# Attention ahead of a mixture of experts on one core: another order of a software pipeline's step, inverses in PSUM, routing by pairs of batches

## The chip, the cores and the metric

The kernel runs on one core of a Trainium2 chip. A core has five engines, each with its own queue that it works through in order: TensorE (PE in the profile, with its weight loads as PEld), VectorE (DVE), ScalarE (ACT), GpSimd (POOL) and SyncE (SP), which here only issues DMAs. The metric is the time on the device in microseconds for one execution, and a kernel's figure is the median over its runs.

## The reference

There are two stages. The first is attention over 8 batches and 8 heads, 576 positions of 64 elements: a local part, in which each position sees its neighbours at a distance under 4, and a pooled part, in which q, k and v are averaged over groups of four positions and the result is repeated four times. The second sends each of the 4608 rows of 512 elements to one of 8 experts.

```python
q_d, k_d, v_d = (t.reshape(B, H, S // 4, 4, D).mean(axis=3) for t in (q, k, v))
out_up = np.repeat(sm_attn(q_d, k_d, v_d), 4, axis=2)
scores = np.where(np.abs(pos[:, None] - pos[None, :]) < 4, scale * q @ k.T, -1e9)
attn = np.exp(scores - scores.max(-1))
attn = attn / (attn.sum(-1) + 1e-9)
x = rows_of(out_up + attn @ v)                   # 4608 x 512
logits = (x / |x|) @ (emb / |emb|).T / tau
e = argmax(logits);  gate = softmax(logits)[e]
out = gate * (relu(x @ w1[e]) @ w2[e])           # w1 512 x 1024, w2 1024 x 512
```

## The kernel before

**Attention** works in 32 units: a batch and a pair of heads, so that two heads of 64 fill 128 partitions. `attention` (line 179) is a software pipeline: in step i, unit a = i + 2 has its keys and queries transposed, unit c = i + 1 gets its scores and exponentials, unit d = i its transposed weights and its products with v, and unit e = i - 1 is turned back into rows. Each engine meets the work in the order in which the code issues it. Per step:

- `qk_T(a)`: 12 transposes on PE (L350) into four PSUM banks, and 8 copies on ACT (L354).
- `scores(c)`: the mask and 36 small products on PE (L383, L388) into one bank, the maximum and the difference on DVE (L394, L395), the exponential on ACT (L396). `scores_d(c)`: the pooled products (L405) into two banks, their maxima on DVE (L409), four exponentials on ACT that also leave their sums (L416).
- `pooled(a)`, `pooled_v(a)`: the sums of four on POOL (L368, L369, L377, L378).
- `weights_T(d)`: 9 transposes (L440) into three banks, copied by ACT (L443). `weights_dT(d)`: 8 transposes (L451) into two banks, copied by DVE (L453).
- `softmax(c)` on DVE: sums (L422), plus 1e-9 (L423), inverses (L424), all in SBUF.
- `rows(e)`: 5 transposes (L491), four into a bank of their own and the fifth into a bank called `shared`; ACT copies the four (L492); the products with the experts' embeddings (L496) into `shared`; DVE copies the fifth (L500) and adds the logits (L502, L504).
- `values_d(d)`: the pooled products with v (L460) into `shared`, copied by ACT (L466). `normalise(c)` on DVE: local weights times inverses (L430, two), pooled weights times inverses (L432). `values(d)`: 18 products with v (L476) into two banks, to which DVE adds the pooled part (L478, two).

All of PSUM is one pool of eight banks that go round: who wants a bank waits until the user eight banks ago has been read out. A step takes 16.

At the end of some steps a part of expert 0's weights is prepared (`first_weights`, line 781): squares on ACT (L748), two a step, or a split into two half-precision parts, ACT (L772) then DVE (L773).

When a batch's last unit is through, `place` (line 507) routes it, in parts that are spread over the following steps: `store` transposes the logits (L530, L531), scales them (L533), copies them into the rows (L534) and saves the rows to DRAM from SP (L519, L520); `pick` finds the first largest logit (L542 to L546); `rank` counts the rows ahead with products on PE (L551, L553) and works out each row's place (L558 to L566), from which POOL makes a table of ones (L568). In total 16 DVE operations a batch. After the first six batches three early slots of rows are gathered within the last steps (`early_slots`).

The loads go from SP, two units (half a batch) at a time: 8 DMAs for k and q (`load`, L316), 2 for v in the layout that is pooled (`load_v`, L325, one buffer), and 10 for v in overlapping windows of 70 positions (`load_w`, L334 for the 64 own rows of each head, L337 for the three rows on either side).

**The experts** (`run_slots`, line 931) work through slots of 128 rows with two products in half-precision parts, L1077 to L1079 and L1100 to L1102.

Of the kernel before, what the change touches and what calls it, by code (L numbers as in the profile page):

```python
# [21 lines left out]
NHP = H // 2  # L22
# [27 lines left out]
class Kern:  # L50
# [128 lines left out]
    def attention(self, ctx):  # L179
# [7 lines left out]
        for i in range(2):  # L187
# [3 lines left out]
            self.vw.append(z.tile([WV, G, 4, D], F32, name=f"vw{i}"))  # L191
            self.sums.append(z.tile([128, G + 4], F32, name=f"sums{i}"))
        self.lg = z.tile([TB, NTB, E + 1], F32, name="lg")
# [27 lines left out]
        for i in range(2):  # L221
            nc.vector.memset(self.kq[i][:, :, :3], 0.0)
            nc.vector.memset(self.kq[i][:, :, S + 3:], 0.0)
            nc.vector.memset(self.vw[i][:32, 0], 0.0)
            nc.vector.memset(self.vw[i][64:, G - 1], 0.0)
# [9 lines left out]
        for i in range(-2, n + 1):  # L235
# [6 lines left out]
            if 0 <= c < n:  # L242
                self.scores(st[c])
                if not c:
                    self.warm_up(3)
                self.scores_d(st[c])
# [8 lines left out]
            if 0 <= d < n:  # L255
                self.weights_T(st[d])
                self.weights_dT(st[d])
                if not d:
                    self.warm_up(7)
            if 0 <= c < n:  # L260
                self.softmax(st[c])
            yield i, 0
            self.shared, last_rows = self.bank(), None
            if mid:
                mid.pop()()
            if 0 <= e < n:
# [4 lines left out]
                last_rows = self.rows(st.pop(e), hp, *xr[b])  # L271
                if hp == NHP - 1:
                    for f in tail:
                        f()
                    tail = self.place(b, *xr.pop(b), mid)
            if 0 <= d < n:
                self.values_d(st[d], last_rows)
            elif last_rows:
                last_rows()
            if 0 <= c < n:  # L280
                self.normalise(st[c])
            if 0 <= d < n:
                self.values(st[d])
# [4 lines left out]
            if tail and i < n:  # L288
                tail.pop(0)()
# [949 lines left out]
```

## Time and profile before

| what | us |
|---|---|
| median of 3 runs | 784.87 (784.14 to 792.7) |
| the profiled execution | 789.27 |
| its span, first to last instruction | 787.6 |
| mean granted TensorE clock | 0.959 |

The profile is of one execution. Busy time counts the instructions of an engine; DMA issues, register and semaphore instructions are left out. The granted clock is the share of TensorE's full clock that it was given. Rows of the timeline give start, duration, engine, line, operation, written tile, read tiles, shape, count, and in brackets how long the engine had been idle before and what ended that. In a group by line, the number after the bar is the busy time, then the mean of one in ns, then the idle time before them. The chain of work that ended last reaches back only over the last 5 us here, so it says nothing of attention.

### The profile page before, as it was taken

The page shows a single profiled execution, that of the slowest core. Times are in us where ns is not written, and L with a number is a line of the kernel's source. Part 1 is how long each engine was busy: PE and PEld are TensorE (multiplying, and loading weights), DVE is VectorE, ACT ScalarE, POOL GpSimd, SP SyncE. Part 2 cuts the span into 40 slices and gives each one's busy share as a digit, 9 for nine tenths or more (in the row PEclk, how much of TensorE's full clock was granted, in tenths as well). Part 3 has the DMA queues.
Part 4 walks back from the last instruction along what each step waited for, and adds up shares of the span by engine and source line. Part 5 has one row for each costly group of instructions (what it writes and reads, how often), then busy time and mean ns, then how long its engine had stood idle before and what let it go on. Part 6 is the DMA issues. An engine that isn't in the chain of part 4 may idle for free. (4 is left out here: it accounts for less than half of the span.)

```text
span 787.6 us, 27918 instructions
## 1 busy us (share of the span) xinstructions
PE 723.7 (92%) x10540; PEld 547.2 (69%) x10540; DVE 508.8 (65%) x1503; ACT 517.0 (66%) x1159; POOL 408.4 (52%) x783
## 2 busy tenths in 40 slices
PE   7899898988998898889999999999999989999992
PEld 4677676767877677657677676777677767776771
DVE  7689799898799987945645647475654364456420
ACT  7698888798888864264754767577583366447510
POOL 7454657475465744726553564565655444525421
PEclk9899999899899978998999999999999999999997
DMA  8788898778789845622833737455553364337210
GB/s 182 144 203 192 194 215 152 222 147 233 135 187 187 169 133 171 184 56 77 254 88 123 192 81 241 120 176 163 189 175 83 83 162 155 83 92 221 60 39 17
DMA packets 160329, 117.77 MB, mean 150 GB/s; under 512 B 90514, under 2 KB 136594, under 8 KB 160160
## 3 DMA queue, kind: packets, MB, share of 16 engines
q1 hardware_dynamic: 152352, 94.55, 49.3%
q0 software_dynamic: 6560, 19.03, 7.9%
q10 hardware_dynamic: 1248, 2.11, 0.8%
q8 instruction: 85, 1.39, 0.8%
q14 instruction: 84, 0.69, 0.3%
HBM read 213.05 MB, written 20.33 MB: 296 GB/s over the span
## 5 line engine op out<-in xcount | busy, mean ns | idle before, releaser
L1077 PE MATMUL bank<-xT,w1h 128*128 128x128 f16 x1312 | 227.2, 221 | 11.1 <-DMA xT<-x 7.8
L1079 PE MATMUL bank<-xT,w1l 128*128 128x128 f16 x1312 | 227.1, 221 | 1.8 <-DVEq L921 1.6
L1078 PE MATMUL bank<-xT,w1h 128*128 128x128 f16 x1312 | 227.2, 221 | 0.0
L1077 PEld LDWEIGHTS <-w1h 128*128 128x128 f16 x1312 | 130.1, 99 | 18.7 <-DMA xT<-x 4.3
L1078 PEld LDWEIGHTS <-w1h 128*128 128x128 f16 x1312 | 130.2, 99 | 3.5
L1079 PEld LDWEIGHTS <-w1l 128*128 128x128 f16 x1312 | 130.1, 99 | 3.3 <-DVEq L921 1.9
L1102 PE MATMUL bank<-w2h,hT 128*128 128x512 f16 x328 | 124.3, 379 | 0.0
L1101 PE MATMUL bank<-w2l,hT 128*128 128x512 f16 x328 | 124.2, 379 | 0.0
L1100 PE MATMUL bank<-w2h,hT 128*128 128x512 f16 x328 | 124.2, 379 | 0.0
L354 ACT ACTIVATE kq<-bank 64x288 f32<-64x288 f32 x256 | 110.1, 430 | 15.4 <-PE bank L350 10.2
L1113 POOL DMA_INDIRECT out_dram<-o,ids x41 | 45.5, 1110 | 126.1 <-ACTq L916 91.9
L1089 DVE SCALAR_TENSOR_TENSOR hT<-bank,hT 128x512 f16<-128x512 f32 x82 | 55.3, 689 | 85.0 <-ACT hT L1088 49.9
L1088 ACT ACTIVATE hT<-bank 128x512 f16<-128x512 f32 x82 | 47.8, 595 | 88.2 <-PE bank L1079 74.8
L368 POOL TENSOR_TENSOR pool_kq<-kq 128x288 f32<-128x288 f32 x62 | 41.7, 680 | 74.0 <-ACT kq L354 71.6
L748 ACT ACTIVATE junk<-st 128x1024 bf16<-128x1024 f32 (+1 forms) x30 | 67.6, 2253 | 3.4 <-issue 2.2
L998 POOL DMA_INDIRECT xg<-xd,ids x41 | 45.5, 1109 | 43.3 <-issue 16.7
L1046 ACT ACTIVATE lg<-lg,lmx 128x8 f32<-128x8 f32 x41 | 12.4, 303 | 74.1 <-DVE lmx L1044 74.1
L377 POOL TENSOR_TENSOR pool_v<-ld_v 72x256 f32<-72x256 f32 x64 | 49.2, 780 | 19.5 <-DMA ld_v<-in_v_dram 17.9
L1102 PEld LDWEIGHTS <-hT 128*128 128x128 f16 x328 | 32.0, 98 | 38.8
L1100 PEld LDWEIGHTS <-hT 128*128 128x128 f16 x328 | 35.0, 107 | 33.9
L1028 DVE SCALAR_TENSOR_TENSOR x<-xg,sc,x 128x512 f16<-128x512 f32 x41 | 30.8, 751 | 40.5 <-ACT x L1025 40.4
L1101 PEld LDWEIGHTS <-hT 128*128 128x128 f16 x328 | 32.0, 97 | 33.9
(218 smaller groups left out, 1604.3 us busy)
## 6 DMA issues: line engine op xcount, KB each, us to landing
st<-in_moe_w_dram SPq DMA_DIRECT2D x148, 1024.0 KB
ld_k<-in_k_dram SPq DMA_DIRECT2D x64, 144.0 KB
ld_q<-in_q_dram SPq DMA_DIRECT2D x64, 144.0 KB
ld_v<-in_v_dram SPq DMA_DIRECT2D x32, 288.0 KB
vw<-in_v_dram SPq DMA_DIRECT2D x64, 144.0 KB
xd<-xr SPq DMA_DIRECT2D x8, 1040.0 KB
st<-in_moe_w_dram SPq DMA_DIRECT2D x12, 512.0 KB
st<-in_moe_w_dram ACTq DMA_DIRECT2D x4, 512.0 KB
```

Source lines behind the costliest of these rows:

```text
L354: nc.scalar.activation(out=kq[h * D:(h + 1) * D, w, 3 + r:3 + r + S:2], in_=ps[r * D:(r + 1) * D], func=AF.Copy, scale=(1.0, QS)[w])
L377: g.tensor_tensor(out=t6[:, c], in0=vr[:, :, 0:2 * D], in1=vr[:, :, 2 * D:], op=ALU.add)
L748: self.nc.scalar.activation(out=junk, in_=src, func=AF.Square, accum_out=acc)
L998: nc.gpsimd.indirect_dma_start(out=xg, out_offset=None, in_=self.xd[:n], in_offset=bass.IndirectOffsetOnAxis(ap=self.ids[:, q:q + 1], axis=0),
L1077: nc.tensor.matmul(out=o, lhsT=self.w1h[:, k, f], rhs=xT[:, 0, k], start=(k == 0), stop=False)
L1078: nc.tensor.matmul(out=o, lhsT=self.w1h[:, k, f], rhs=xT[:, 1, k], start=False, stop=False)
L1079: nc.tensor.matmul(out=o, lhsT=self.w1l[:, k, f], rhs=xT[:, 0, k], start=False, stop=(k == self.KC - 1))
L1088: nc.scalar.activation(out=h[:, 0], in_=ps, func=AF.Relu)
L1089: nc.vector.scalar_tensor_tensor(out=h[:, 1], in0=ps, scalar=0.0, in1=h[:, 0], op0=ALU.max, op1=ALU.subtract)
L1100: nc.tensor.matmul(out=ps, lhsT=hh, rhs=self.w2h[:, j, :], start=(j == 0), stop=False)
L1101: nc.tensor.matmul(out=ps, lhsT=hh, rhs=self.w2l[:, j, :], start=False, stop=False)
L1102: nc.tensor.matmul(out=ps, lhsT=hl, rhs=self.w2h[:, j, :], start=False, stop=(j == self.FC - 1))
```

## The change

- The order within a step. `scores` and `scores_d` now hold the products alone; the maxima and exponentials became `exps`, `peaks_d` and `exps_d`. PE does `weights_T(d)` before `scores_d(c)`. ACT copies the transposed weights (before: L443) ahead of the exponentials. After the row transposes, the order of DVE is: the row copies, `softmax`, the additions of `values`, and `normalise` last. ACT's copy of the rows (L492) comes after that of the pooled products (L466).
- PSUM: seven banks go round, and the eighth holds the inverses: the sums stay in SBUF, the sum plus 1e-9 and the inverse are written to PSUM, and `normalise` reads them there.
- Routing: for the first six batches `place` only does `store`, and every second batch `place_pair` does the rest for two batches at once, in seven parts, one a step (two a step in the four steps after batch 5). `store`'s copy into the rows, the products of `pick` and `rank` and one difference go to POOL. The parts are issued before the row transposes, where they stood at the end of the step.
- Loads of v: `load_v` is one DMA, `load_w` three (the own rows of four heads at once, and three rows on either side at once, in which rows of a neighbouring head come in where the weights are zero). The pooled positions are now split into even and odd ones instead of halves, so `weights_dT` reads every second column.

```diff
+            if 0 <= c < n:
+                self.scores_d(st[c])
+                self.exps(st[c])
+                self.peaks_d(st[c])
+            if 0 <= d < n:
                 self.weights_dT(st[d])
             if 0 <= c < n:
-                self.softmax(st[c])
+                self.exps_d(st[c])
             yield i, 0
-            self.shared, last_rows = self.bank(), None
             if mid:
                 mid.pop()()
+            for _ in range(2 if BEARLY * NHP <= i < (BEARLY + 1) * NHP else 1):
+                if tail and i < n:
+                    tail.pop(0)()
+            self.shared, parts = self.bank(), None
...
+            if 0 <= d < n:
+                self.values_d(st[d])
+            if parts:
+                parts[1]()
+            if 0 <= c < n:
+                self.softmax(st[c])
+            if 0 <= d < n:
+                self.out_d(st[d])
+                self.values(st[d])
+            if parts:
+                parts[0]()
...
             if 0 <= c < n:
                 self.normalise(st[c])
...
-        vr = ld.tile([CD, 2, 4, 4 * D], F32, name="ld_v", bufs=1)
-        for c in range(2):
-            nc.sync.dma_start(out=vr[:, c], in_=self.v[b, h, c * S // 2:(c + 1) * S // 2].rearrange(
-                "h (i r) d -> i h (r d)", r=4))
+        vr = ld.tile([CD, 4, 2, 4 * D], F32, name="ld_v", bufs=1)
+        nc.sync.dma_start(out=vr, in_=self.v[b, h].rearrange("h (i c r) d -> i h (c r d)", c=2, r=4))
...
-        for c in range(4):
-            own = bass.AP(g.tensor, g[c, 0:1].offset, [[D, 64], [64 * D, G], [1, D]])
-            nc.sync.dma_start(out=vw[3:WV - 3, :, c], in_=own)
-        for p, w0, t0 in [(r, 1, 61 + r) for r in range(3)] + [(WV - 3 + r, 0, 64 + r) for r in range(3)]:
-            edge = bass.AP(g.tensor, g[0, t0:t0 + 1].offset, [[D, 1], [64 * D, G - 1], [S * D, 4], [1, D]])
-            nc.sync.dma_start(out=vw[p:p + 1, w0:w0 + G - 1], in_=edge)
+        for p, np, f0, nf, t0 in ((3, 64, 0, n, 0), (0, 3, 1, n - 1, 61), (WV - 3, 3, 0, n - 1, 64)):
+            rows = bass.AP(g.tensor, g[0, t0:t0 + 1].offset, [[D, np], [64 * D, nf], [1, D]])
+            nc.sync.dma_start(out=vw[p:p + np, f0:f0 + nf], in_=rows)
...
-        nc.vector.tensor_scalar(out=sums, in0=sums, scalar1=1e-9, scalar2=None, op0=ALU.add)
-        nc.vector.reciprocal(out=sums, in_=sums)
+        inv = self.inv[:, s["u"] % 2]
+        nc.vector.tensor_scalar(out=inv, in0=sums, scalar1=1e-9, scalar2=None, op0=ALU.add)
+        nc.vector.reciprocal(out=inv, in_=inv)
...
-                nc.tensor.transpose(out=pt[:, i * CD:(i + 1) * CD], in_=s["ad"][:, i, c * CD:(c + 1) * CD],
+                nc.tensor.transpose(out=pt[:, i * CD:(i + 1) * CD], in_=s["ad"][:, i, c::2],
...
-            v.tensor_copy(out=xr[:, :, DM:], in_=lg[:, :, :E])
+            (v if b == B - 1 else nc.gpsimd).tensor_copy(out=xr[:, :, DM:], in_=lg[:, :, :E])
...
+        if b < BEARLY:
+            mid.append(store)
+            return self.place_pair(b - 1) if b % 2 else []
...
+    def place_pair(self, b0):
...
+        def best():
+            v.reduce_max(out=mx, in_=l8, axis=AX.X)
+            v.tensor_tensor(out=l8, in0=l8, in1=bc(mx), op=ALU.is_ge)
+            for i in range(2):
+                g.tensor_tensor(out=l8[:, i], in0=l8[:, i], in1=self.rev, op=ALU.mult)
+        def first():
+            v.reduce_max(out=mx, in_=lg, axis=AX.X)
+            v.tensor_tensor(out=oh[:, :, :NTB], in0=l8, in1=bc(mx), op=ALU.is_equal)
+        def rank(i):
...
+        def own():
+            for i in range(2):
+                g.tensor_tensor(out=rk[:, i], in0=rk[:, i], in1=oh[:, i, :NTB], op=ALU.mult)
...
+        def split():
+            v.reduce_sum(out=pos, in_=rk, axis=AX.X)
+            v.tensor_copy(out=posi, in_=pos)
+            v.tensor_scalar(out=posi, in0=posi, scalar1=SLOT - 1, scalar2=None, op0=ALU.bitwise_and)
+            v.tensor_copy(out=pm, in_=posi)
+            g.tensor_tensor(out=pb, in0=pos, in1=pm, op=ALU.subtract)
+            at(0)
+        return [best, first, lambda: rank(0), lambda: rank(1), own, split, lambda: at(1)]
...
-        self.bk = self.pool(ctx, "banks", 8, space=PSUM)
+        self.bk = self.pool(ctx, "banks", 7, space=PSUM)
+        self.inv = self.pool(ctx, "inverses", 1, space=PSUM).tile([128, 2, G + 4], F32, name="inv")
```

More of the change, by code (lines that the diff above doesn't have):

```diff
@@ L270, in attention @@
                              self.rt.tile([128, LW], F32, name="ls"))
-                last_rows = self.rows(st.pop(e), hp, *xr[b])
-                if hp == NHP - 1:
[L273 to L279, printed above, removed]
+                parts = self.rows(st.pop(e), hp, *xr[b])
+            if 0 <= d < n:
[9 more added lines that the diff above has]
+                parts[0]()
+                if hp == NHP - 1:
+                    while tail and b >= BEARLY:
+                        tail.pop(0)()
+                    tail += self.place(b, *xr.pop(b), mid)
+                    if b == B - 2:
+                        tail.pop(0)()
             if 0 <= c < n:
                 self.normalise(st[c])
-            if 0 <= d < n:
-                self.values(st[d])
             if i == -1:
@@ L374, in pooled_v @@
         t6 = wk.tile([CD, 2, 2, 2 * D], F32, name="pool_v", bufs=1)
-        for c in range(2):
-            vr = s["v"][:, c, j:j + 2]
-            g.tensor_tensor(out=t6[:, c], in0=vr[:, :, 0:2 * D], in1=vr[:, :, 2 * D:], op=ALU.add)
+        for h in range(2):
+            vr = s["v"][:, j + h]
+            g.tensor_tensor(out=t6[:, h], in0=vr[:, :, 0:2 * D], in1=vr[:, :, 2 * D:], op=ALU.add)
         g.tensor_tensor(out=vd, in0=t6[:, :, :, 0:D], in1=t6[:, :, :, D:], op=ALU.add)
@@ L497, in rows @@
                              start=True, stop=True)
+        def first():
+            nc.scalar.activation(out=dst[:, :4], in_=ps, func=AF.Copy)
         def rest():
@@ L504, in rest @@
                 nc.vector.tensor_copy(out=ls, in_=lg)
-        return rest
+        return first, rest
     def place(self, b, xr, ls, mid):
@@ L540, in pick @@
             l8 = lg[:, :, :E]
-            mx = rt.tile([TB, NTB], F32, name="lmx")
+            mx = rt.tile([TB, 2, NTB], F32, name="lmx2")[:, 0]
             v.reduce_max(out=mx, in_=l8, axis=AX.X)
@@ L575, in place, with bc, first, at @@
         return [take, pick, rank]
+    def place_pair(self, b0):
+        nc, rt = self.nc, self.rt
+        v, g = nc.vector, nc.gpsimd
+        bs = slice(b0, b0 + 2)
+        lg, oh = self.lg, self.oh[:, bs]
+        l8, shp = lg[:, :, :, :E], [TB, 2, NTB, E]
+        mx = rt.tile([TB, 2, NTB], F32, name="lmx2")
+        rk = rt.tile(shp, F32, name="rk2")
+        pos = rt.tile([TB, 2, NTB], F32, name="pos2")
+        posi = rt.tile([TB, 2, NTB], I32, name="posi2")
+        pm, pb = self.pm[:, bs], self.pb[:, bs]
+        def bc(x):
+            return x.unsqueeze(3).broadcast_to(shp)
+        def best():
[3 more added lines that the diff above has]
+                g.tensor_tensor(out=l8[:, i], in0=l8[:, i], in1=self.rev, op=ALU.mult)
+        def first():
+            v.reduce_max(out=mx, in_=lg, axis=AX.X)
+            v.tensor_tensor(out=oh[:, :, :NTB], in0=l8, in1=bc(mx), op=ALU.is_equal)
+        def rank(i):
+            pk, o = self.bank()[:, :(NTB + 1) * E].rearrange("p (t e) -> p t e", e=E), oh[:, i]
+            nc.tensor.matmul(out=pk, lhsT=self.tri, rhs=o, start=True, stop=False)
+            for t in range(1, NTB + 1):
+                nc.tensor.matmul(out=pk[:, t:], lhsT=self.onesb, rhs=o[:, :NTB + 1 - t], start=False,
+                                 stop=(t == NTB))
+            v.tensor_tensor(out=rk[:, i], in0=pk[:, :NTB], in1=self.base.unsqueeze(1).broadcast_to(shp[:1] + shp[2:]),
+                            op=ALU.add)
+            v.tensor_tensor(out=self.base, in0=self.base, in1=pk[:, NTB], op=ALU.add)
+        def own():
+            for i in range(2):
+                g.tensor_tensor(out=rk[:, i], in0=rk[:, i], in1=oh[:, i, :NTB], op=ALU.mult)
+        def at(i):
+            for t in range(NTB):
+                g.tensor_scalar(out=self.at[:, (b0 + i) * NTB + t], in0=self.iota, scalar1=pm[:, i, t:t + 1],
+                                scalar2=None, op0=ALU.is_equal)
+        def split():
[6 more added lines that the diff above has]
+        return [best, first, lambda: rank(0), lambda: rank(1), own, split, lambda: at(1)]
```

54 lines of the change are left out of this document (30 added, 24 removed).

## The prediction

> **What bounds the kernel now.** I read the page first, then the table of stretches, then the timeline of one step, then groups by line.
>
> ```profile
> span 787.6 us, 27918 instructions
> PE 723.7 (92%) x10540; PEld 547.2 (69%) x10540; DVE 508.8 (65%) x1503; ACT 517.0 (66%) x1159; POOL 408.4 (52%) x783
> ```
>
> TensorE is busy 92% of the span, but that is an average over two stages. The table below cuts attention at the starts of its steps (the first transpose L350 of a unit). The columns are span, then busy time and count of PE, PEld, DVE, ACT and POOL, then granted clock, DMA share and GB/s.
>
> ```profile
> 36.20:77.00 40.80, 38.00 (x846) 31.14 (x844) 36.49 (x101) 36.83 (x112) 18.93 (x27) 1.00 0.83 186
> 97.30:131.70 34.40, 30.67 (x679) 24.93 (x678) 31.79 (x87) 30.18 (x90) 23.28 (x30) 1.00 0.88 186
> 151.30:186.80 35.50, 30.86 (x682) 25.01 (x681) 32.51 (x84) 31.24 (x91) 21.70 (x28) 1.00 0.79 185
> 208.00:267.80 59.80, 53.17 (x1188) 43.26 (x1187) 54.80 (x150) 53.17 (x157) 35.14 (x50) 1.00 0.87 180
> 77.00:97.30 20.30, 17.09 (x342) 13.63 (x339) 15.13 (x41) 18.61 (x52) 12.27 (x18) 0.92 0.85 201
> 131.70:151.30 19.60, 18.62 (x343) 15.40 (x342) 16.35 (x42) 15.60 (x46) 8.75 (x13) 0.83 0.86 210
> 186.80:208.00 21.20, 19.65 (x343) 15.75 (x339) 15.02 (x42) 18.77 (x52) 13.31 (x19) 0.76 0.83 185
> 267.80:278.00 10.20, 8.63 (x170) 6.98 (x167) 9.66 (x25) 8.51 (x25) 8.93 (x9) 0.89 0.73 122
> 306.90:787.60 480.70, 452.29 (x5082) 330.52 (x5082) 248.38 (x787) 261.97 (x423) 229.97 (x520) 0.98 0.45 130
> ```
>
> From 306.9 us the experts run with PE busy 94%, and the change adds or removes nothing there but a PSUM bank. So the change acts on attention. The first four rows are 20 steps at full clock, 170.5 us or 8.5 each; the next four are 7 steps, 71.3 us, at a lower clock. At full clock no engine is full: ACT needs 7.4 a step (36.83 over 5), DVE 7.3 to 8.1, PE 7.6. A chain through all of them sets the step. Here is one, 8.23 us long, with only its carriers:
>
> ```profile
> 114.15 0.45 PE L350 MATMUL bank<-ident,ld_k 96*128 96x96 f32 x3
> 114.69 3.57 ACT L354 ACTIVATE kq<-bank 64x288 f32<-64x288 f32 x8 [0.66 <-PE bank L350]
> 115.23 0.81 DVE L478 TENSOR_TENSOR xT<-bank,od 128x320 f32<-128x320 f32 x2
> 116.19 0.71 PE L405 MATMUL bank<-kqd 64*72 64x144 f32 x8
> 116.83 1.18 PE L440 MATMUL bank<-ident,an 128*70 128x128 f32 x9
> 117.96 0.52 DVE L395 TENSOR_TENSOR a<-bank,mx 128x342 f32<-128x342 f32 x1
> 118.57 0.49 ACT L396 ACTIVATE a<-a 128x342 f32<-128x342 f32 x1 [0.30 <-DVE a L395]
> 119.08 0.38 ACT L416 ACTIVATE ad<-bank,md 72x144 f32<-72x144 f32 x1
> 119.97 0.33 PE L491 MATMUL bank<-ident,xT 128*128 128x128 f32 x1 [0.72 <-ACT ad L416]
> 120.53 1.24 ACT L443 ACTIVATE aT<-bank 70x384 f32<-70x384 f32 x3
> 121.23 1.22 PE L476 MATMUL bank<-aT,vw 70*64 70x64 f32 x36
> 121.92 1.73 DVE L430 TENSOR_TENSOR an<-a,sums 64x342 f32<-64x342 f32 x2
> 122.38 0.47 PE L350 MATMUL bank<-ident,ld_k 96*128 96x96 f32 x3
> ```
>
> Read it as a ring. L350 starts; 0.54 later ACT copies keys and queries for 3.57; ACT waits 0.30 for DVE; the exponentials of the local part and half of the pooled part take until 119.9 (118.57 on); then the fifth transpose L491 gets its bank, which those pooled exponentials were reading (0.72 of PE idle); from there PE runs on, 119.97 to 122.38, and the next L350 begins. The copies L443 stand behind the exponentials on ACT although PE had their data by 118.0 (L440).
>
> **The change, part by part.**
>
> *Order on ACT and banks.* L443 goes ahead of the exponentials, the pooled scores go behind the weight transposes on PE, and 7 banks rotate instead of 8. A step still takes 16 banks, so each waits for the one 7 uses back: the first bank of the weight transposes L451 now waits for the last L354, and the row transposes L491 for L443, done early. The new ring is L350, 0.54, L354 3.57, a semaphore (0.05), then PE alone from L451 to the next L350. An undisturbed stretch of that kind is in the trace:
>
> ```profile
> 300.46 0.67 PE L451 MATMUL bank<-ident,ad 72*72 72x72 f32 x8
> 302.61 1.22 PE L476 MATMUL bank<-aT,vw 70*64 70x64 f32 x36
> ```
>
> L451 to L476 is 2.15, and L476 to the next L350 1.15 (121.23 to 122.38) to 1.22: 3.4. So the ring is 0.54 + 3.57 + 0.05 + 3.4 = 7.6, against ACT's own 7.4. In a step with a piece of expert weights, ACT has one split more and is the bound.
>
> ```profile
> L748 ACT ACTIVATE junk<-st 128x1024 bf16<-128x1024 f32 x8 | 8.5, 1061 | 0.1
> L772 ACT ACTIVATE w1h<-st,wscl 128x1024 f16<-128x1024 f32 x4 | 4.7, 1166 | 0.0
> L773 DVE SCALAR_TENSOR_TENSOR w1l<-st,wscl,w1h 128x1024 f16<-128x1024 f32 x4 | 5.1, 1268 | 0.0
> L430 DVE TENSOR_TENSOR an<-a,sums 64x342 f32<-64x342 f32 x60 | 37.3, 621 | 0.4
> L395 DVE TENSOR_TENSOR a<-bank,mx 128x342 f32<-128x342 f32 x29 | 14.9, 515 | 1.0
> L543 DVE TENSOR_TENSOR lg<-lg,lmx 128x40 f32<-128x40 f32 x7 | 1.4, 200 | 0.2
> ```
>
> That is 7.4 + 1.1 = 8.45 rounded; DVE's 1.27 is then covered, since routing and L430 become cheaper (below). Of the 20 steps at full clock I count 15 plain, 5 with a split, and 1.6 us of PE waiting for its own instructions that I leave: 15 x 7.6 + 5 x 8.45 + 1.6 = 157.8, a gain of 12.7. The 7 others are held by a half clock or by two squares on ACT (2 x 1.061 a step), which stay; I take 0.4 each, half of a plain step's 0.9, so 2.9. Together 15.6.
>
> *Inverses in PSUM, normalisation last.* L430 had two SBUF operands and averages 621 ns; L395, as wide with one operand in PSUM, 515. L430 stretches to 1.73 for two (121.92) where POOL adds beside it, and L395 keeps its price. I take 515; 621 is the other end. Both lie beside PE's work: PE's L476 ends with the step, so the last of two L478 (0.81) and two L430 (1.03) end at most 1.9 later, and L440 wants them 2.0 after the first L350 (116.83 less 114.15, less the 0.64 of L405, which now follows it). If it is late, the first 0.5 is free: PE gets to L451 at about 3.6 and waits there for L354 until 4.16.
>
> The last two steps have no L350 and no L354 to cover that: L440 is wanted 1.0 earlier in one and at once in the other. I take 1.0 + 1.4 = 2.4 lost.
>
> *Routing by pairs.* For six batches, two routings of 13 DVE operations become one of 12 for the pair, at 200 ns (L543): some 3 us less DVE a pair, where DVE isn't the ring, so nothing by itself. But the copy of the logits into the rows goes to POOL, and the comparison that overwrites these logits follows it on DVE in the same step.
>
> ```profile
> 102.30 0.82 DVE L453 COPY adT<-bank 72x288 f32<-72x288 f32 x2
> 104.37 0.73 POOL L378 TENSOR_TENSOR vd<-pool_v 72x256 f32<-72x256 f32 x1
> ```
>
> In that step, begun at 97.3, DVE was through with L453 5.8 in, and POOL, whose queue holds the pooling ahead of the copy, with L378 7.8 in. So DVE is held some 2 us, with the row copies, L422, L478 and L430 behind it, and PE's next L440 behind those. The store's transposes put PE back by 0.4, and 0.5 falls into L451's wait: 1.1 a time, for batches 1 and 3. For the last pair two parts share a step: once the comparison, two products on POOL and the maximum (five operations of 0.2 more: 2.2), once the products and the split, with nothing else to shift PE (2.5). Together 6.9. POOL's own additions, a copy and some products of 40 elements, fit in the time in which it waits for ACT. SP's save of the batch now waits for POOL's copy, and the eight key and query loads of the next half but one stand behind it; they have two steps left before they are wanted: zero.
>
> *Fewer loads.* Of v, twelve issues become four a half. All issue on SP and nothing waits on `vw`; nor does the landing of `ld_v` reach PE. Zero, with both ends below a microsecond a half. The transposes L451 read every second column, which no row shows. Ends: nothing, or L451 doubled (0.67 a step, 21 us). I take nothing: L476, nearest to it, reads blocks with gaps, 36 in 1.22.
>
> *Eighth bank.* The experts use four banks a slot, so seven still reach back over a slot: zero.
>
> **Sum.** 15.6 - 2.4 - 6.9 = 6.3. The profiled execution took 789.27 (span 787.6 and 1.67 around it) and would take 783.0; the median 784.87 becomes 778.6.
>
> **The rivals.** *The clock drops go too.* The half clock starts after a poorly filled 3.41 us.
>
> ```profile
> 125.65:129.06 3.41, 2.16 (x20) 1.61 (x18) 3.38 (x7) 2.41 (x8) 3.33 (x4) 1.00 0.57 147
> 129.06:132.47 3.41, 3.22 (x63) 2.73 (x64) 2.70 (x8) 3.41 (x12) 2.48 (x4) 1.00 1.19 265
> 190.50:193.91 3.41, 2.02 (x16) 1.32 (x16) 2.86 (x7) 3.29 (x12) 3.41 (x7) 1.00 1.01 210
> 193.91:204.15 10.24, 10.24 (x153) 8.30 (x153) 5.73 (x14) 9.18 (x27) 5.57 (x8) 0.50 0.58 111
> ```
>
> PE was busy 2.02 of 3.41, nearly all transposes and waits, then ran 10.24 at 0.50. Attention has nine such 3.41 us stretches after 40 us; each costs up to 1.7. The new order puts the pooled scores between two groups of transposes and takes the 0.72 wait out; if six of nine stretches go, at 1.0 each as those steps have other limits, the time is 772. Against it: the waits of 1.1 to 2.5 before L440 can set off new ones, and I count those equal. The Trainium skill, "TensorE: Matmul & The Clock Gate", § Part 4, says that transposes do not count as PE's business for the clock; by that rule most drops would go. The trace fits it at 190.5 and not at 125.65, where transposes alone filled 2.16 and the clock stayed at 1.00 (first two rows).
>
> *The feed bounds instead.* DMA share is 0.88 at 8.6 us a step; at 7.9 it would be 0.95. If it stops near 0.9 the steps keep their length, and the waits fall into them: 786. For it, POOL waits on `ld_v` today; against it, no PE wait on a load in these stretches, and a share above 1.0 in 190.5 to 193.91.
>
> *Slower: L451 reads at half pace.* It lies on the new ring, behind L354, so its whole price counts: 0.67 more in each of 32 steps is 21 us, 800. It decides from 0.44 a step (14 us, the far side of 1%). For it, no transpose here reads with a gap between elements; against it, L476. The Trainium skill, "SBUF — State Buffer", § Door 1 (its note on cachelines), lets consecutive accesses that share a 16-byte line run at full pace, as two of these do; no run here shows it.
>
> **How the numbers follow.** The forecast (773 to 785) has 0.48, clock drops gone or the POOL waits hidden (764 to 773) 0.24, the feed (785 to 791) 0.16, slower (over 792.7) 0.12. This measurement can tell about 1%, 7.8 us: faster means below 777.0. That is 0.24 and 0.18 of the forecast's 0.48: 0.42. Slower is 0.12, and 0.46 remains. The range 766 to 791 leaves out the slower cases and the best end; the forecast's own is 773 to 785.
>
> **What would show it.** Right: plain steps of 7.6, L443 directly behind L354, no L491 waiting on L416, L451 waiting for L354 about 0.5; four steps, for pairs of batches, in which DVE idles 2 us for POOL and the next L440 waits for DVE. Wrong: L451 of some 1.3 (slower), plain steps still above 8 with SP or DMA ahead of L350 (feed), or DVE passing the comparison unheld (nearer 772).

## The result and the profile after

The changed kernel took 799.06 us in the median of 4 runs (795.22 to 801.59), the kernel before 786.5 beside it: 1.011 of it, interval 1.006 to 1.016. Measured again with the experiments, it took 1.019 (1.015 to 1.024). So it is slower by 1 to 2%, where 0.8% faster was forecast (778.6 against 784.87). The profiled execution took 799.08 us.

```profile
span 797.4 us, 27764 instructions
PE 740.3 (93%) x10540; PEld 556.4 (70%) x10540; DVE 487.3 (61%) x1454; ACT 514.3 (65%) x1159; POOL 396.4 (50%) x805
```

PE does the same 10540 matmuls and is busy 16.6 us longer; DVE does less, as meant. The table of stretches shows where. Columns as in the prediction; first the kernel before, from 40 us to the experts and then the last stretch of that, from the last unit's first transpose L350 on:

```profile
40.00:306.90 266.90, 238.29 (x4910) 193.31 (x4909) 232.18 (x635) 226.81 (x659) 153.76 (x213) 0.94 0.81 182
278.00:306.90 28.90, 25.39 (x454) 20.54 (x451) 24.04 (x79) 17.05 (x49) 11.95 (x21) 0.85 0.49 154
```

The changed kernel in the same stretches, and its experts:

```profile
40.00:319.70 279.70, 254.24 (x4844) 201.54 (x4843) 208.95 (x567) 221.33 (x645) 143.98 (x235) 0.88 0.82 172
283.60:319.70 36.10, 29.73 (x452) 22.53 (x451) 25.21 (x80) 17.71 (x50) 16.48 (x30) 0.71 0.39 123
319.70:797.40 477.70, 451.19 (x5086) 329.85 (x5082) 248.86 (x788) 261.15 (x423) 227.06 (x516) 0.98 0.47 131
```

Attention is 12.8 us longer, the experts 3.0 shorter. In attention PE's idle time, span less busy, went from 28.6 to 25.5 us: the change does take waits away. But PE's busy time went from 238.3 to 254.2 at a granted clock of 0.88 instead of 0.94. Busy time multiplied by clock is 224 in both: about the same work (4910 matmuls in this stretch before, 4844 after), at a lower clock. 7.2 of the 12.8 us lie in the last stretch. The clock of the other executions says the same: in those on which the ratios rest, span multiplied by granted clock is on average 759.2 us for the kernel before (77 executions of the four rounds of experiments, mean span 787.6, mean clock 0.964) and 759.4 for the changed one (9 executions, 800.4 and 0.949). As an estimate, at equal clock the two kernels would take the same time. The waits of PE behind these sums, before:

```profile
PE bank L491 <- ACT ad L416: 13.7, 22, 0.8
PE bank L388 <- issue: 4.9, 6, 1.8
PE bank L451 <- ACT kq L354: 3.0, 9, 0.4
```

and after, where L350 has become L359, L354 L363, L430 L455, L440 L465, L443 L468, L451 L476, L466 L491, L491 L516 and L534 L560:

```profile
PE bank L465 <- DVE an L455: 11.1, 20, 3.4
PE bank L397 <- issue: 4.4, 4, 2.2
PE bank L359 <- ACT od L491: 2.2, 2, 1.2
PE bank L419 <- ACT kq L363: 2.1, 9, 0.4
```

The numbers are the total, how often, and the longest. The wait of the row transposes on the pooled exponentials, 22 times and never over 0.8, is gone, as forecast. In its place PE waits for the normalised weights, 11.1 us in total instead of 13.7, but up to 3.4 us at a time. What waits do to the clock, in three places of the changed kernel (a full stretch of 3.41 us, then what followed):

```profile
83.57:86.98 3.41, 2.05 (x37) 1.20 (x23) 2.09 (x5) 3.30 (x9) 0.03 (x1) 1.00 0.96 197
86.98:100.63 13.65, 13.65 (x171) 11.11 (x173) 7.29 (x21) 9.18 (x27) 6.32 (x10) 0.50 0.84 140
168.90:172.31 3.41, 1.59 (x15) 1.18 (x13) 1.76 (x6) 2.76 (x12) 3.19 (x5) 1.00 0.89 287
172.31:182.55 10.24, 10.24 (x153) 8.39 (x154) 5.40 (x15) 5.62 (x14) 3.20 (x7) 0.50 0.96 284
308.85:312.26 3.41, 1.64 (x22) 1.67 (x23) 3.02 (x10) 1.54 (x5) 2.13 (x8) 1.00 0.01 2
312.26:322.50 10.24, 10.24 (x102) 7.67 (x100) 6.08 (x25) 3.39 (x8) 3.52 (x8) 0.50 0.15 27
```

PE was busy 1.59 to 2.05 of 3.41 us and then ran 10 to 14 us at half clock, fully busy. The waits in the three differ: in the first four of 0.26 to 0.41 us, in the second one of 1.82 for PE's own instructions, in the third one of 2.33 of L465 for DVE. From 40 us to the experts half clock adds up to 65.5 us (31.1 before); as half of it is lost, the difference is worth 17 us: more than attention lost, as PE's idle time got shorter.

Two places of the changed kernel in which DVE waited for POOL: above the dots the last pair, below them batch 6, in the last stretch; rows of POOL, DVE and PE by start:

```profile
253.17 0.24 DVE L625 TENSOR_TENSOR lg<-lg,lmx 128x80 f32<-128x80 f32 x1 [1.60 <-POOL xr L560]
254.01 0.25 DVE L630 TENSOR_REDUCE lmx<-lg 128x10 f32<-128x90 f32 x1 [0.60 <-POOL lg L627]
255.46 0.47 PE L359 MATMUL bank<-ident,ld_q 96*128 96x96 f32 x3 [0.98 <-ACT od L491]
257.78 1.04 PE L465 MATMUL bank<-ident,an 128*70 128x128 f32 x4 [0.75 <-DVE an L455]
...
292.78 1.29 POOL L1083 DMA_INDIRECT xg<-xd,ids  x1 [0.32 <-DVE lg L559]
294.38 1.00 POOL L1083 DMA_INDIRECT xg<-xd,ids  x1 [0.30 <-issue]
295.68 1.00 POOL L1083 DMA_INDIRECT xg<-xd,ids  x1 [0.30 <-issue]
296.69 0.22 POOL L560 COPY xr<-lg 128x40 f32<-128x40 f32 x1
296.94 0.20 DVE L569 TENSOR_TENSOR lg<-lg,lmx 128x40 f32<-128x40 f32 x1 [3.94 <-POOL xr L560]
301.22 2.11 PE L465 MATMUL bank<-ident,an 128*70 128x128 f32 x9 [3.38 <-DVE an L455]
```

The last pair is as forecast in kind: DVE idles 1.60 and 0.60 for POOL, PE then twice. In batches 1 and 3, where about 2 us were forecast, DVE idled 0.10 each in this execution, in which both steps ran partly at half clock; in a second profiled execution it idled 1.53 and 1.60, and PE 0.75 each behind it. Not forecast: POOL's copy of batch 6's logits stood behind three gathers of rows, DVE idled 3.94 us for it, and PE 3.38 for DVE.

### The profile page after: what moved, and what is told of

The parts are those of the page before. It is cut to its first block, busy times and chain, and to the rows that moved or that the text cites. A ratio compares the mean times of both kernels' runs of the same rounds, so it can differ in the third digit from the quotient of the medians.

```text
span 797.4 us, 27764 instructions
## 1 busy us (share of the span) xinstructions
PE 740.3 (93%) x10540; PEld 556.4 (70%) x10540; DVE 487.3 (61%) x1454; ACT 514.3 (65%) x1159; POOL 396.4 (50%) x805
## 5 line engine op out<-in xcount | busy, mean ns | idle before, releaser
L363 ACT ACTIVATE kq<-bank 64x288 f32<-64x288 f32 x256 | 109.5, 428 | 9.9 <-PE bank L359 5.5
L1083 POOL DMA_INDIRECT xg<-xd,ids x41 | 45.5, 1109 | 41.7 <-POOLq L1007 13.7
L68 POOL TENSOR_SCALAR nw_t<-nw_y,nw_a 128x1 f32<-128x1 f32 x120 | 49.8, 415 | 12.1
L386 POOL TENSOR_TENSOR pool_v<-ld_v 72x256 f32<-72x256 f32 x64 | 45.2, 724 | 21.1 <-DMA ld_v<-in_v_dram 21.0
```

What stands on the lines that cost most here:

```text
L68: g.tensor_scalar(out=t, in0=y, scalar1=y, scalar2=a, op0=ALU.mult, op1=ALU.mult)
L363: nc.scalar.activation(out=kq[h * D:(h + 1) * D, w, 3 + r:3 + r + S:2], in_=ps[r * D:(r + 1) * D], func=AF.Copy, scale=(1.0, QS)[w])
```

## The experiments

Each kernel was timed beside the kernel before; the ratio is to that, with its 95% interval. The columns behind it are of one profiled execution, from 40 us to the experts: span, PE's busy time, its granted clock, its idle time (span less busy), and the time at half clock (granted clock 0.5).

| kernel | ratio | span | PE busy | clock | idle | half |
|---|---|---|---|---|---|---|
| before | 1 | 266.9 | 238.3 | 0.94 | 28.6 | 31.1 |
| changed, first time | 1.011 (1.006 to 1.016) | 279.7 | 254.2 | 0.88 | 25.5 | 65.5 |
| changed, second time | 1.019 (1.015 to 1.024) | 279.9 | 256.4 | 0.88 | 23.5 | 65.9 |
| order | 0.999 (0.995 to 1.002) | 260.4 | 230.3 | 0.97 | 30.1 | 17.1 |
| old loads | 1.011 (1.003 to 1.018) | 274.7 | 239.6 | 0.94 | 35.1 | 30.7 |
| no POOL | 0.999 (0.995 to 1.004) | 266.1 | 242.8 | 0.94 | 23.3 | 32.0 |
| copy of batch 6 | 1.004 (0.999 to 1.008) | 270.6 | 247.2 | 0.92 | 23.4 | 44.4 |
| eight banks | 1.006 (1.002 to 1.011) | 268.2 | 240.2 | 0.92 | 28.0 | 42.1 |
| eight banks, no POOL | 0.998 (0.993 to 1.002) | 265.6 | 239.0 | 0.93 | 26.6 | 35.1 |
| the same, early normalising (columns of the second) | 0.984 (0.979 to 0.990), 0.995 (0.991 to 0.999) | 261.6 | 236.6 | 0.94 | 25.1 | 31.8 |
| the same, routing behind the normalising | 1.000 (0.996 to 1.004) | 264.0 | 239.7 | 0.94 | 24.3 | 30.7 |
| changed, early normalising (columns of an execution of 804.03, the median is 796.99) | 1.005 (1.001 to 1.009) | 271.9 | 247.2 | 0.93 | 24.7 | 39.0 |
| order, early normalising | 1.001 (0.997 to 1.005) | 261.4 | 228.7 | 0.99 | 32.7 | 6.8 |
| old routing | none, see there | 274.3 | 247.4 | 0.92 | 27.0 | 44.4 |
| waits filled (columns of an execution of 813.94, the median is 811.25) | 1.020 (1.012 to 1.027) | 282.0 | 253.9 | 0.91 | 28.1 | 48.7 |
| six long waits in before | 1.048 (1.042 to 1.054) | 309.2 | 259.3 | 0.83 | 49.9 | 105.8 |
| six short waits in before | 1.028 (1.022 to 1.033) | 282.8 | 246.6 | 0.90 | 36.2 | 56.5 |

### The order of the step alone

The kernel before with the new functions and the new order of the loop; eight banks, inverses in SBUF, routing and loads as before.

```diff
 (on the kernel before)
+                self.scores_d(st[c])
+                self.exps(st[c])
+                self.peaks_d(st[c])
...
+            if parts:
+                parts[1]()
+            if 0 <= c < n:
+                self.softmax(st[c])
+            if 0 <= d < n:
+                self.out_d(st[d])
+                self.values(st[d])
+            if parts:
+                parts[0]()
...
```

> The kernel before with the new order of a step alone: eight banks, inverses in SBUF, routing batch by batch with its copy on DVE, the old loads of v. Theory POOL (the loss sits in routing, where DVE stands behind POOL's queue): the order alone is a gain, 8 to 14 us below the kernel before, and plain steps take 7.8 to 8.0 us. Theory clock (the new order itself leads to longer stretches at half clock, 68 us between 40 and 330 us in the changed kernel against 34 before): no gain or a loss, 0 to 8 us above the kernel before, with the half-clock time above 50 us. Theory loads: as POOL here, a gain of 8 to 14 us.

Measured 0.999, not slower, and with less half clock than before (17.1 us). The three steps without routing or weights took 7.53 to 7.56, what the ring promised (7.6), the later ones 7.9 to 9.5. PE's waits:

```profile
PE bank L465 <- DVE an L455: 11.8, 13, 2.3
PE bank L485 <- DVE adT L478: 10.7, 14, 1.2
```

The wait on ACT became waits on DVE, which still has the routing of each batch; idle time is 30.1 against 28.6. So the order by itself neither brings the time up nor wins more than it hands on. Attention was 6.5 us shorter, of which the experts gave back 3.3 (484.0 against 480.7 us): PE waited for gathered rows 12.0 us there, against 7.8 before.

### Old routing, old loads, no POOL

The changed kernel with one part undone: routing of each batch by itself on DVE, at the end of a step; or `load_v`, `load_w` and the pooled halves as before; or the pair routing kept, but POOL's copy and products done by DVE.

```diff
 (no POOL)
-            (v if b == B - 1 else nc.gpsimd).tensor_copy(out=xr[:, :, DM:], in_=lg[:, :, :E])
+            v.tensor_copy(out=xr[:, :, DM:], in_=lg[:, :, :E])
...
-                g.tensor_tensor(out=l8[:, i], in0=l8[:, i], in1=self.rev, op=ALU.mult)
+                v.tensor_tensor(out=l8[:, i], in0=l8[:, i], in1=self.rev, op=ALU.mult)
...
-                g.tensor_tensor(out=rk[:, i], in0=rk[:, i], in1=oh[:, i, :NTB], op=ALU.mult)
+                v.tensor_tensor(out=rk[:, i], in0=rk[:, i], in1=oh[:, i, :NTB], op=ALU.mult)
```

> The changed kernel with routing batch by batch as before (all on DVE), all else as changed. Theory POOL: the 12 us over the kernel before go and more, some 5 to 10 us below the kernel before; DVE has no wait on POOL's copy at batch 6 (3.9 us there) nor at the last pair (1.6 and 0.6). Theory clock: still 5 us or more above the kernel before. Theory loads: 5 us or more above the kernel before.

> The changed kernel with the loads of v as before (two and ten DMAs a half, v pooled by halves), all else as changed. Theory loads (the few large DMAs hold up instruction fetches, and PE's waits for its own instructions of 1.6, 1.8 and 2.2 us start the half clock): back to the kernel before or below it, 0 to 10 us faster than it. Theory POOL: stays within 4 us of the changed kernel, 8 to 14 us above the kernel before. Theory clock: the same 8 to 14 us above.

> The changed kernel with the pair routing kept, but the copy of the logits and the products with the ranks on DVE instead of POOL (only the subtraction and the tables stay on POOL). Theory POOL: 8 to 16 us faster than the changed kernel, so at the kernel before or up to 5 us below it. Theory clock: 0 to 4 us faster than the changed kernel. Theory loads: no more than 4 us faster than the changed kernel.

Without POOL's part the loss is gone: 0.999. Idle time hardly differs (23.3 against 25.5 and 23.5), but half clock falls from 65.5 to 32.0 us. With the old loads the ratio is that of the changed kernel, 1.011, but the time goes elsewhere: half clock is as in the kernel before (30.7), and PE's idle time is 35.1, some 10 us more than in the changed kernel, 4.8 of it waits on loads and up to 5.8 at a time waits of the weight transposes for DVE. So the fewer loads do save waits on loads here, and why the changed kernel loses as much by its clock instead isn't shown. The old routing's four runs lay between 784.25 and 803.45; they allow no verdict. In its one profile attention is 274.3 us and half clock 44.4, with waits of PE for its own instructions of up to 3.7 us.

### The copy of batch 6

```diff
-            (v if b == B - 1 else nc.gpsimd).tensor_copy(out=xr[:, :, DM:], in_=lg[:, :, :E])
+            (v if b >= BEARLY else nc.gpsimd).tensor_copy(out=xr[:, :, DM:], in_=lg[:, :, :E])
```

> The changed kernel with one line altered: the copy of the logits of batch 6 is done by DVE, like that of batch 7, while the first six batches keep POOL's. In the changed kernel that copy stood behind three gathers of token rows on POOL (1.29, 1.00 and 1.00 us from 292.78 on), DVE idled 3.94 us for it, and L465 came 3.38 us late. Theory POOL: DVE no longer idles there, L465 follows at once, the stretch from the last step's first matmul to the experts goes from 36.1 us back to about 31 (before: 28.8), and the ratio to the kernel before falls from 1.011 to about 1.005. Theory clock: the length of that stretch is made by the half clock of 291.8 to 305.4, the wait only lies in it; then the stretch stays at 34 or more unless the half clock goes as well, and the ratio stays above 1.008.

Rows of this kernel's timeline at the same place:

```profile
288.69 0.20 DVE L569 TENSOR_TENSOR lg<-lg,lmx 128x40 f32<-128x40 f32 x1
289.94 1.00 POOL L1083 DMA_INDIRECT xg<-xd,ids  x1 [0.30 <-issue]
294.03 2.10 PE L465 MATMUL bank<-ident,an 128*70 128x128 f32 x9
```

DVE no longer waits for the gathers, L465 follows without a wait, and the last stretch fell from 36.1 us to 32.0. The ratio is 1.004 (0.999 to 1.008), 0.7 to 1.5% below the two figures of the changed kernel. By these middle values this one line is half or more of POOL's share; the interval overlaps with that of the first figure.

### Eight banks and inverses in SBUF

```diff
-        self.bk = self.pool(ctx, "banks", 7, space=PSUM)
-        self.inv = self.pool(ctx, "inverses", 1, space=PSUM).tile([128, 2, G + 4], F32, name="inv")
+        self.bk = self.pool(ctx, "banks", 8, space=PSUM)
...
+        self.inv = self.cp.tile([128, 2, G + 4], F32, name="inv")
```

> The changed kernel with part B undone: 8 rotating banks instead of 7, and sums and inverses in SBUF instead of PSUM. All waits on POOL stay. Theory bank (the eighth bank was not free, as the forecast had it): steps at full clock without routing go from 7.8 to 8.0 back to the 7.55 that the order alone showed, some 4 us in all, and the waits on ACT's copy od in the steps after the routing (0.98 and 1.25) go; ratio about 1.006. Theory inverse (the inverses in PSUM save DVE time in each step): DVE's two products of the weights go from 1.02 back to as much as 1.7 beside POOL, L465 waits longer, steps of 8.2 and more; ratio 1.012 or above. Theory POOL alone: neither matters, steps and ratio stay at 1.011.

> Both at once: no copy and no product of the routing on POOL, 8 rotating banks, inverses in SBUF; what stays of the change is the new order of the step, the routing of two batches together, and the fewer loads of v. POOL alone took the ratio to 0.999. Theory bank: another 3 to 4 us, ratio 0.994 to 0.996, attention part about 302 us (the order alone: 300.4). Theory POOL alone: ratio 0.999 as without the bank, attention part 306. Theory inverse: slower than without the bank, ratio 1.002 or above.

A step of the changed kernel without expert weights, 7.92 us:

```profile
139.12 0.47 PE L359 MATMUL bank<-ident,ld_k 96*128 96x96 f32 x3
139.68 3.57 ACT L363 ACTIVATE kq<-bank 64x288 f32<-64x288 f32 x8
141.52 1.15 PE L465 MATMUL bank<-ident,an 128*70 128x128 f32 x9 [0.27 <-DVE an L455]
142.60 0.71 PE L419 MATMUL bank<-kqd 64*72 64x144 f32 x8
143.28 1.24 ACT L468 ACTIVATE aT<-bank 70x384 f32<-70x384 f32 x3
143.31 1.00 PE L476 MATMUL bank<-ident,ad 72*72 72x72 f32 x8
144.19 0.77 PE L516 MATMUL bank<-ident,xT 128*128 128x128 f32 x5
147.04 0.47 PE L359 MATMUL bank<-ident,ld_k 96*128 96x96 f32 x3
```

and one of the same kernel with eight banks, 7.54:

```profile
50.72 0.47 PE L359 MATMUL bank<-ident,ld_k 96*128 96x96 f32 x3
53.07 1.15 PE L465 MATMUL bank<-ident,an 128*70 128x128 f32 x9 [0.22 <-ACT kq L363]
54.80 0.77 PE L476 MATMUL bank<-ident,ad 72*72 72x72 f32 x8
55.41 0.76 PE L516 MATMUL bank<-ident,xT 128*128 128x128 f32 x5
58.26 0.38 PE L359 MATMUL bank<-ident,ld_k 96*128 96x96 f32 x2
```

From L476 to L516 it is 0.88 with seven banks and 0.61 with eight: with seven banks the second four transposes of L476 wait for the first of ACT's three copies L468, which begin at 143.28, and the row transposes L516 for the second; each starts 0.05 after that copy ends. So the eighth bank was worth some 0.3 in such a step; the ratio fell to 1.006, though against the first figure of the changed kernel the intervals overlap. Without POOL's part the eighth bank makes no difference that shows (0.998 against 0.999).

The inverses are another matter. The products with them by group, before, after, and after with eight banks and the inverses in SBUF:

```profile
L430 DVE TENSOR_TENSOR an<-a,sums 64x342 f32<-64x342 f32 x58 | 36.3, 625 | 0.4
```

```profile
L455 DVE TENSOR_TENSOR an<-a,inv 64x342 f32<-64x342 f32 x58 | 29.2, 503 | 0.4
```

```profile
L455 DVE TENSOR_TENSOR an<-a,inv 64x342 f32<-64x342 f32 x58 | 29.9, 515 | 0.4
```

Read alone, these groups say that the new place in the step took 110 ns off and PSUM another 12. But the order alone has the new place too, with inverses in SBUF, and its products average 610. The difference is POOL. A pair of products beside POOL's sums of v, in the order alone (SBUF), then with the old routing (PSUM):

```profile
119.10 1.68 POOL L386 TENSOR_TENSOR pool_v<-ld_v 72x256 f32<-72x256 f32 x2
119.42 1.73 DVE L455 TENSOR_TENSOR an<-a,inv 64x342 f32<-64x342 f32 x2
```

```profile
117.61 1.42 POOL L383 TENSOR_TENSOR pool_v<-ld_v 72x256 f32<-72x256 f32 x2
117.99 1.02 DVE L452 TENSOR_TENSOR an<-a,inv 64x342 f32<-64x342 f32 x2
```

With inverses in SBUF, products beside an addition of POOL took 752 ns on average before (28 of 58) and 825 in the order alone (19 of 58), the others 506 and 505. With inverses in PSUM they took 504 beside POOL (20 of 58, old routing) and 505 elsewhere. So PSUM does take the stretching away. With eight banks and inverses in SBUF it doesn't show, because there none of the 58 products met an addition of POOL.

### What a wait of PE costs

In the kernel before, 16 (or 8) memsets of DVE on a spare tile, ahead of the normalising of six units:

```diff
+        if s["u"] in (5, 9, 13, 17, 21, 25):
+            for _ in range(16):
+                nc.vector.memset(self.pad, 0.0)
```

> The kernel before, with 16 memsets of DVE on a spare tile (128x256, about 0.27 us each, 4.3 us in all) ahead of the normalising of the units 5, 9, 13, 17, 21 and 25: six waits of PE for DVE, 2 to 3 us each, in an otherwise unchanged kernel. It measures what a wait of PE costs by itself. Theory wait alone: the time grows by what PE idles at L440 more, W in the profile, 12 to 18 us; half clock between 40 and 330 us stays near the 34 us of before. Theory clock (a wait is followed by half clock, which costs as much again): the time grows by at least 1.4 W, and the half clock between 40 and 330 us grows to 55 or more.

> The kernel before with 8 memsets of DVE (2.15 us) instead of 16 ahead of the normalising of the units 5, 9, 13, 17, 21 and 25; with 16 the waits of PE were 3.6 to 6.5 us, so now about 1.4 each in the four later steps, 8 to 14 us in all. Theory every wait halves the clock: half clock between 40 us and the experts at 70 us or more, time plus 1.5 times the waits, ratio 1.016 to 1.027. Theory threshold (only waits of some 2 us or more do): half clock below 50 us, ratio at most 1.014.

With 16, the six waits and the half clock around one of them:

```profile
PE bank L406 <- DVE xT L482: 26.6, 6, 6.5
```

```profile
143.59:147.00 3.41, 2.16 (x23) 1.36 (x25) 3.02 (x9) 2.47 (x11) 3.08 (x5) 1.00 1.08 229
147.00:150.41 3.41, 3.41 (x48) 3.29 (x45) 2.26 (x9) 2.69 (x6) 1.46 (x2) 0.50 1.11 224
150.41:160.65 10.24, 6.66 (x100) 5.06 (x99) 8.97 (x20) 3.90 (x10) 6.95 (x6) 0.50 0.66 117
```

The waits are not the expected ones, of L440 for the normalised weights, but of the pooled products for a bank that DVE's additions (here L482) still had to read. 26.6 us of waits cost 41 us (832.02 against 791.01), 1.5 times their length, and half clock rose to 105.8 us. In two of the six places the drop follows the wait (at 61.67 and 112.87). In the other four, as here, it came ahead of the memsets (they begin at 148.14), after a stretch in which several waits under 0.8 added up to 1.25; there the wait only kept the clock low. With 8 memsets, PE's idle time rose by 7.6 us, half clock to 56.5, and the time by some 21: more than twice the idle time. Neither expectation was met: half clock lies between the two (70 or more, below 50), the ratio at the upper end of the first. The memsets also held up POOL (4.6 us of PE waits on its sums), so that figure is not of the waits alone.

### Filling the waits

14 unused matmuls ahead of L465 in four late steps of the changed kernel.

> The changed kernel with 14 more matmuls of 128x512 on zeroed or spare weights (0.25 us each at full clock by the pair that took 1.03 us at half clock), put ahead of the transposes L465 of four steps where PE waited: two each in the steps of values 26 and 28, six in 30 (wait of 3.38), four in 31 (wait of 2.33). They compute nothing that is used. Theory clock (the clock halves after a stretch with little PE work, and that holds the loss): the half clock of 291.8 to 305.4 and of 312.3 to 322.5 goes or shrinks, the last stretch goes from 36 to about 31, the whole from 799 to about 793. Theory POOL: the waits end no earlier, so the last stretch keeps its 36 or gains at most 2; the matmuls that lie outside a wait add up to 1 us.

In the profiled execution the last stretch shrank (32.9 us at a clock of 0.88, against 36.1 at 0.71), which speaks for the clock; but the time did not: 1.020 (1.012 to 1.027), no better than the changed kernel. PE waited up to 3.4 us for its own instructions elsewhere, and the experts took 490.2 us instead of 477.7. No gain, and no proof.

### The last two steps, and the routing behind the normalising

Sums, inverses and weights normalised directly behind the exponentials in the last two steps; on the changed kernel, on the one without POOL and with eight banks (twice), and on the order alone. Last, the same with the pair routing moved behind the normalising.

```diff
             if 0 <= c < n:
                 self.exps_d(st[c])
+            if n - 2 <= c < n:
+                self.softmax(st[c])
+                self.normalise(st[c])
...
```

> The changed kernel, except that in the last two steps sums, inverses and weights are normalised directly behind the exponentials, ahead of the routing of batch 6 and of the copies and sums of the step (as far as the order of ACT allows). POOL keeps all its copies and products. Theory tail (the new place of the normalising, last in the step, is what the two last steps cannot cover): the waits of L465 on DVE of 3.38 and 2.33 go almost wholly, also behind the gathers, and the stretch from the last qk_T to the experts goes from 36.1 to 29 to 31; ratio 1.003 to 1.005, as with batch 6's copy on DVE or better. Theory POOL alone: the copy behind the gathers still holds up DVE, now behind the normalising, and the wait shows up at the values or the rows; at most 2 us are gained, ratio 1.008 or above.

> The same early normalising in the last two steps, with no copy or product of the routing on POOL, 8 banks and inverses in SBUF. Without the early normalising this was 0.998 of the kernel before, with 6.0 us of waits of L465 on DVE in the last stretch of 34.9. Theory tail: waits below 1 us there, stretch 29 or less, ratio 0.991 to 0.993. If half clock and not the waits makes that stretch: still 33 or more, ratio 0.997.

> The kernel without POOL's part in the routing, with 8 banks, inverses in SBUF and early normalising in the last two steps, a second time. Theory tail: 0.984 to 0.990 again. If the first five runs were a draw of luck: 0.994 to 0.998, as without the early normalising.

> The kernel before with the new order of the step alone, and early normalising in the last two steps; old routing, old loads. The order alone was 0.999 with a last stretch of 31.3 us, one wait of L465 of 2.3 us and half clock of 13.7 us in it. Theory tail: the wait goes, the last stretch comes to 28 or 29, ratio 0.990 to 0.995. Rival (the order's gain is lost in the experts, where PE waited 12.0 us for gathered rows instead of 7.8, as they depend on the end of POOL's and the queue's work and not on PE): the attention part ends 2 us earlier and the experts take as much longer; ratio 0.997 or above.

> As the run before, and the parts of the pair routing stand behind the normalising at the end of a step instead of ahead of it (none in the step in which a batch ends). Theory routing ahead of the normalising (it stands between the exponentials and the weights that PE waits for): L465 of the steps k28 and k30 (values 27 and 29) no longer waits 1.2 and 1.5 us for DVE, these steps take 9.0 to 9.3 as with the order alone instead of 9.8 and 10.0, and the steps 12, 17 and 20 come to 7.6 to 8.2; about 2 to 3 us in all, ratio 0.988 to 0.991. Rival: the work behind the normalising delays the reading of the next scores (L408) by as much, and adT with it; no gain, ratio as in the run before.

> The changed kernel as it is, on the chip of the three runs beside it. Expected 1.007 to 1.015 of the kernel before (first measured: 1.011 in 4 runs); its profile again has half clock of 40 us or more between 40 us and the experts, and the last stretch (last qk_T to experts) of 33 us or more.

On the changed kernel 1.005 (1.001 to 1.009), about as the copy of batch 6. Without POOL and with eight banks 0.984, and when measured again 0.995 (0.991 to 0.999): faster than the kernel before, by something between 0.1 and 2%. On the order alone 1.001 (0.997 to 1.005): nothing, though no wait over 1.4 us is left in the last stretch and it ran at full clock throughout. So what the last two steps lose by the new place of the normalising is not shown to be more than the 2.4 us forecast. With the routing moved, the three steps behind the last pair took 26.8 us instead of 28.2, but the ratio is 1.000 (0.996 to 1.004): in the last stretch PE then waited 2.1 us for POOL's table of ones and 2.0 for DVE.

## Why the prediction was wrong

The forecast was 778.6, the time 799.06: 20 us, of which 1.6 are the kernel before itself (786.5 beside it instead of 784.87).

- **The clock: the step that failed.** The prediction saw that half clock starts after a poorly filled 3.41 us, and that the new waits "can set off new ones", and counted drops gone and drops new as equal. They went from 31.1 to 65.5 us (65.9 in a second profile), 17 us of loss. It had the mechanism and the waits in hand, and put zero. That POOL's part brings the loss is shown for the kernel as a whole: without it half clock is 32.0 and the loss gone. Which wait sets off which drop is not shown. In the changed kernel's profile 23.9 us of half clock (from 86.98 and 192.79) follow four waits under 0.42 in one stretch, and the kernel without POOL's part has two such drops as well (from 79.53 and 185.34); 13.7 (from 172.31 and 230.34) follow waits of PE for its own instructions; 6.8 (from 257.64 and 274.71) lie beside the last pair's waits on POOL; 13.7 begin at 291.78, 1 us ahead of batch 6's gathers; the last 7.4 follow L465's 2.33.
- **Routing by pairs: the term of 6.9 was too small, as one wait was missed and the clock left out.** The prediction took in POOL's pooling ahead of the copy, in batches 1 and 3 and in the last pair; for batch 6, which is routed alone, the three gathers stand there. That wait alone was 3.94, and the measured share of POOL is 1.2% of the first ratio and 2.0% of the second, 9 to 16 us. For the last pair 2.2 and 2.5 were forecast; DVE idled 2.2 in one step and 2.5 in the other. For batches 1 and 3, at 1.1 each, PE waited 0.75 each in the second profile, and DVE's wait was 0.10 in the first. POOL also reached PE over a way that was not foreseen: the held-up `od` keeps its bank, for which L359 waits twice, 2.2 in all.
- **The order of the step: 7.6 forecast, 7.8 to 7.9 measured,** and 8.8 to 9.2 for 8.45. The ring was right, and is there with eight banks (7.54). "The first bank of L451 waits for the last L354" was right too. What failed is "the row transposes L491 for L443, done early": the copies (now L468) stand behind the last L363 on ACT and begin at 143.28, so the row transposes and the second bank of L476 wait for them, 0.27 a step. The wait of L465 on DVE of 0.27 did disappear behind L363, as forecast. The eighth bank was put at zero on the experts' account alone. In the sum, 7 x 0.4 is 2.8 and not 2.9, which changes nothing.
- **The last two steps:** in the last, L465 waited 2.33 where 1.4 was the figure. In the one ahead of it, 3.38 where 1.0 was the figure, the wait is batch 6's: with that copy on DVE it is gone. More is not shown.
- **Inverses in PSUM:** the mechanism was right. 515 ns were taken and 503 measured, and the stretching of L430 beside POOL goes with PSUM, as the old routing shows.
- **Fewer loads** at zero: not borne out, as with the old loads PE waits 4.8 us on them and idles some 10 us more in all; in the time it doesn't show. Reading every second column costs nothing: L476 takes 0.77 for eight undisturbed, where 0.67 to 0.87 were L451's. So the rival of 800 gave the right time by a mechanism that isn't there; the feed of DMAs, the other one, is not seen either, with no wait of PE on a load from 40 us on.
- **The clock drops go too**, the rival of 772, went the other way. Its seed is in the order alone: 17.1 us of half clock.

## What to carry to other kernels

Do not add up waits: ask how much of them falls into one stretch of 3.41 us, in one piece or in four. In this kernel waits cost 1.5 times their length and more, because the clock drops behind them, or stays low through them. One trace in which two units of work do not meet says nothing of what they do when they meet: the products and POOL's additions needed a kernel in which they overlap. Before work moves to another engine's queue, list everything that stands ahead of it there at each of its places, and the odd one out first (here the batch that is routed alone). A PSUM bank taken from a ring is priced at every user of the ring, the second of two banks as well as the first.

## What the runs showed of the hardware

I divided the 18 traces of this study into whole stretches of 3.41 us along the grid on which the granted clock changes, from 40 us to the experts, and took those at full clock:

| PE busy in the stretch | stretches | half clock in the next |
|---|---|---|
| under 1.6 us | 30 | 30 |
| 1.6 to 2.4 us | 110 | 52 |
| over 2.4 us | 1064 | 13 |

So idle time of over 1.8 us in one stretch, in one wait or several, was followed by half clock all 30 times, and 1.0 to 1.8 about every other time. Nine of the 13 in the last row, with PE busy 2.9 to 3.2, lie at one place in nine of the traces: they hold 30 short products with POOL's table of ones in the last steps (from 289.47 in the changed kernel). In three of these nine POOL has no copy of the routing, and what lowers the clock there stays open. The clock came back in 89 cases, each behind a stretch with PE busy over 2.8 us, but in 39 only behind the third or a later one. The Trainium skill, "TensorE: Matmul & The Clock Gate", § Why this matters for your kernels, asks for no idle gaps over about 3 us; by these traces 1.0 to 1.8 us in a stretch can be too much, and in several pieces. The same page of the Trainium skill, § Part 4, says that a transpose doesn't count as busy time of PE in the same way. Of 42 stretches with under 0.5 us of other work than transposes 22 were followed by half clock: all 15 with PE busy under 1.6 us, 6 of 14 with 1.6 to 2.4, and 1 of 13 above. So by these traces PE's whole busy time is the better measure.

PE also waited for its own instructions, 0.4 to 10.0 us of attention in sum, at places that change with the code (up to 2.2 us at a time in the changed kernel, none over 0.41 with the order alone); what decides that stays open.
